# Moving vector work, loads and sums about in a TensorE-bound attention-and-experts kernel

## The chip, the cores and the metric

The kernel runs on one core of a Trainium2 chip. The metric is the device time of one execution in microseconds (us), the median of several runs; lower is better. Engines are named as the profile names them: PE is TensorE (PEld its weight loads), DVE is VectorE, ACT is ScalarE, POOL is GpSimd, SP is SyncE, which here only issues DMAs. The 16 runs of the kernel before lie within 0.4% of one another.

## The reference, cut to what matters

```python
def reference(...):
    # q, k, v: (8 batches, 8 heads, 576 tokens, 64), float32
    # sliding-window attention (window 128) with a distance bias per head
    x = attention(q, k, v)                  # then reshaped to 4608 tokens x 512
    logits = x @ w_gate                     # 8 experts
    P = exp(logits - logits.max())
    for _ in range(8):                      # Sinkhorn: rows and columns in turn
        P /= P.sum(1, keepdims=True) + 1e-09
        P /= P.sum(0, keepdims=True) + 1e-09
        P *= N / E
    out = 0
    for e in range(8):                      # every token goes to every expert
        h = maximum(x @ w1[e], 0)           # 512 -> 1024
        out += P[:, e:e+1] * (h @ w2[e])    # 1024 -> 512
    return out
```

Two facts follow from it. Routing weights need all tokens (column sums), so Sinkhorn cannot start before attention ends. And the eight dense experts are the bulk of the work.

## The kernel before

The kernel has these stages in time:

1. Attention, block by block, with expert 0 filled in wherever TensorE has room. Expert 0 does not need routing weights before its output is scaled, so six of its nine groups of 512 tokens are done here. Activations of a group are also written to DRAM (`xTd`), from where later experts read them.
2. Sinkhorn on VectorE and GpSimd, while TensorE does the other three groups of expert 0. The routing weights then go through DRAM (`PTd`) and come back broadcast to all partitions (`Pb`).
3. Expert 1, nine tasks of one group each, then experts 2 and 3, 4 and 5, 6 and 7 in pairs. Both layers use a Strassen (Winograd) form: seven products of half-size blocks for eight, paid for with sums and differences on VectorE. The names below: `xd` sums of activations, `ws` sums of first-layer weights, `T` sums of second-layer weights, `S` sums of hidden activations. A call `chunk(j, n)` is one eighth of the first layer of task `j`; it is woven into the second layer of the task before.

The result accumulates in `acc` in SBUF. `quad(g, rh, ch)` is one quarter (256 token rows by 256 columns) of a group. In the Winograd form one partial sum belongs to three of the four quarters: it is kept once, in quarter (1,1), and added to the others at the end (`settle`). For that, expert 0's result has to be scaled by its routing weight (`rescale`) and quarter (1,1) subtracted from two other quarters (`rebase`).

```python
        # Sinkhorn stage: four weight loads (2 MB in DRAM each), then eight iterations
        load_w1(1, msb); load_w2(1, msb); load_w1(2, msb); load_w2(2, msb)   # issued by GpSimd
        for it in range(ITERS):
            ...                                   # row sums on VectorE
            nc.gpsimd.partition_all_reduce(ca_sb, cs_sb, P, bass_isa.ReduceOp.add)
            ...
        for g in range(g0):                       # g0 = 6
            rebase(g, 1)                          # VectorE, 128x512
        load_x(f"0_{g0}", g0)                     # activations of groups 6 and 7 from DRAM
        load_x(f"0_{g0 + 1}", g0 + 1)
        e0_l1(g0)                                 # expert 0, first layer, group 6
        for g in range(g0 + 1, NG):
            e0_l1(g)
            if g < NG - 1:
                e0_l2(g - 1)
        # (cut) transposes of the routing weights -> PT_sb -> DRAM (PTd)
        e0_l2(NG - 2)
        load_w1(3, per)
        # (cut) read PTd back as Pb; weight sums of expert 1; first chunks between e0_l2(NG - 1)
        load_w2(3, per)
```

```python
    # (cut) inside an expert-1 task h; order = (1, 7, 5, 6, 2, 4, 3)
    for k in range(7):
        unit.product(order[k])                    # 8 matmuls of 256 columns
        chunk(j, k if k < 4 else k + 1)           # 8, 8, 8 or 4 matmuls of the next task, in turn
        if k == 0:
            unit.make_s(2)
            unit.gather(0)                        # VectorE: quarter (1,1) += product 1
        if k == 1: unit.gather(1, op=ALU.subtract)
        if k == 2: unit.gather(2, op=ALU.subtract)
        if k == 3: unit.gather(3)
        if k == 4:
            unit.make_s(4)
            unit.gather_far(0, 0, 0)              # ScalarE copy + accumulating DMA
        # (cut) k == 5, 6: two more gather_far; make_x of the task after next
        if k in (0, 1, 2, 4):
            rescale(4 * (h + 1) + (0, 1, 2, None, 3)[k])      # ScalarE, 128x512
        if k == 5:
            rebase(h + 1, 0)                      # VectorE, 128x512
            if h + 1 >= g0:
                rebase(h + 1, 1)
```

```python
    # weight sums and T tiles at a change of experts (h = first task of the expert)
    at(h - 2, 3, make_ws, e, 1); at(h - 2, 5, make_ws, e, 2)
    at(h - 2, 6, make_ws, e, 3); at(h - 1, 0, make_ws, e, 4)
    at(h, 3, make_t, p, 0); at(h, 6, make_t, p, 3)            # for pairs after the first
    at(h + 1, 1, make_t, p, 1); at(h + 1, 6, make_t, p, 2)
```

The softmax here doesn't subtract the row's maximum and nothing guards it: scores larger than these inputs give would overflow.

## Time and profile before

| | before |
|---|---|
| median, 16 runs | 1072.34 us (1069.83 to 1074.42) |
| profiled span | 1071.1 us |
| TensorE busy | 94% |
| attention ends (last gate matmul) | 211.1 us |
| first expert-1 product | 274.0 us |
| last matmul starts | 1061.3 us |

The first line is from the page of the kernel before: busy time of each engine, its share of the span, and instructions.

```profile
PE 1007.3 (94%) x9187; PEld 818.0 (76%) x9187; DVE 861.5 (80%) x1352; ACT 645.2 (60%) x1154; POOL 204.6 (19%) x211
```

94% looks full, but shares over the span say little here. The stage windows say more. Columns of the window view: stretch in us, its length, then busy time and (instructions) of PE, PEld, DVE, ACT, POOL, then the granted TensorE clock, the busy share of the DMA engines and their GB/s. The lines are of the kernel before.

```profile
275.00:300.00 25.00, 24.74 (x225) 21.64 (x223) 23.18 (x38) 20.27 (x37) 4.84 (x4) 1.00 0.48 112
300.00:325.00 25.00, 24.27 (x218) 20.89 (x217) 23.58 (x38) 20.09 (x37) 7.19 (x6) 1.00 0.60 117
325.00:350.00 25.00, 23.93 (x216) 20.64 (x214) 23.58 (x38) 19.88 (x37) 6.17 (x6) 1.00 0.63 126
350.00:375.00 25.00, 23.20 (x207) 19.81 (x205) 23.77 (x39) 19.44 (x36) 7.02 (x6) 1.00 0.64 127
375.00:400.00 25.00, 20.78 (x179) 17.19 (x178) 23.83 (x37) 15.93 (x29) 5.57 (x5) 1.00 0.64 137
400.00:425.00 25.00, 22.90 (x207) 19.93 (x205) 22.32 (x30) 14.03 (x25) 3.53 (x4) 1.00 0.71 138
...
450.00:475.00 25.00, 25.00 (x232) 22.40 (x230) 20.22 (x29) 15.40 (x29) 3.98 (x4) 1.00 0.42 96
...
600.00:625.00 25.00, 24.06 (x219) 21.10 (x217) 23.67 (x36) 14.62 (x27) 4.89 (x6) 1.00 0.93 180
```

Read the count beside the busy time of PE. In the steady paired stage (450 us) TensorE is busy 25.00 of 25 us and starts 232 matmuls. Up to 425 us it starts fewer, down to 179, while DVE is busy 22.3 to 23.8 us. Busy time alone hides part of this, because matmuls overlap: 218 against 232 matmuls is 6% less work, 24.27 against 25.00 us is 3%.

The length of one expert-1 task can be read from the SyncE timeline: it issues one load of `Pb` per task. Columns: start, duration, engine, line, operation, out<-in.

```profile
324.04 0.42 SPq L579 DMA_DIRECT2D Pb<-PTd  x1
337.30 0.42 SPq L579 DMA_DIRECT2D Pb<-PTd  x1
```

That is 13.26 us a task here (12.65 us in the tasks without a weight sum).

Between attention and expert 1 the waits of PE from 210 to 275 us, kernel before (waiter, line, what it waited for: us in total, times, longest), are:

```profile
PE psh L114 <- DMA xl<-xTd: 7.1, 1, 7.1
PE la L641 <- DVE xl L586: 2.6, 1, 2.6
```

And the chain that ended last, kernel before, runs through the DRAM round trip of the routing weights (start, us, what):

```profile
249.54 6.64 DMA PTd<-PT_sb
...
256.20 4.10 DMA Pb<-PTd
...
260.52 1.24 DVE xl L586
...
261.85 0.60 PE la L641 x4
```

The end of the kernel before, from its timeline. In brackets stands the idle time before and what ended it.

```profile
1045.71 20.70 SPq L76 DMA_DIRECT2D out_dram<-acc_hi  x20
...
1055.45 0.69 DVE L780 TENSOR_TENSOR acc_hi<-acc_hi 128x512 f32<-128x512 f32 x1 [2.82 <-DMA acc_hi<-st]
...
1057.93 1.92 PE L741 MATMUL M<-w2t,S 128*128 128x256 f16 x16 [3.13 <-DVE S L721]
...
1061.33 5.39 ACTq L76 DMA_DIRECT2D out_dram<-acc_hi  x4
```

A `settle` (L780) waits 2.8 us for an accumulating DMA, the last S tile stands behind it on VectorE, and TensorE waits 3.1 us for that tile. SyncE is still issuing stores at 1066.4 us.

### The profile page before, as it was taken

The numbers are of one execution on the slowest core, as the hardware profiler recorded it, in microseconds if no ns is written. First come the engines' busy times: TensorE is split into PE (matmuls) and PEld (weight loads), VectorE is DVE, ScalarE is ACT, GpSimd is POOL, SyncE is SP. The second block draws the span as 40 slices with busy tenths as digits, with TensorE's granted clock in tenths as the row PEclk, the third lists the DMA queues.
The fourth block names the chain that finished last, engine by engine and source line by source line (L and its number), as shares of the span: only waits on it lengthen the run. The fifth ranks groups of instructions, "written<-read, shape, count | busy, mean of one in ns | idle before, by whom it ended". The sixth has DMA issues, their size and how long they took to land.

```text
span 1071.1 us, 22451 instructions
## 1 busy us (share of the span) xinstructions
PE 1007.3 (94%) x9187; PEld 818.0 (76%) x9187; DVE 861.5 (80%) x1352; ACT 645.2 (60%) x1154; POOL 204.6 (19%) x211
## 2 busy tenths in 40 slices
PE   4899999789999989999999999999999999999995
PEld 2555555434788768888888888888888888888884
DVE  5777767565999998888888997888888988888874
ACT  3576666445787765665656555666655565655660
POOL 6323230020122221111111211111111111111111
PEclk9799999989999999999999999999999999999999
DMA  9977883194666566445334983344446635555545
GB/s 174 168 96 91 103 106 39 41 213 110 128 119 119 119 137 130 100 111 106 90 89 97 182 176 90 89 94 96 109 109 137 129 89 129 149 138 129 129 108 139
DMA packets 122071, 125.98 MB, mean 118 GB/s; under 512 B 46704, under 2 KB 97424, under 8 KB 121968
## 3 DMA queue, kind: packets, MB, share of 16 engines
q0 software_dynamic: 92720, 58.89, 40.0%
q1 hardware_dynamic: 28960, 65.40, 19.9%
q8 instruction: 72, 1.18, 0.5%
q10 hardware_dynamic: 288, 0.26, 0.1%
q14 instruction: 31, 0.25, 0.1%
HBM read 113.62 MB, written 14.30 MB: 119 GB/s over the span
## 4 chain that ended last, share of the span: by engine, by line
issue 58%; PE 21%; POOL 12%; DMA 3%; DVE 3%; ACT 2%; POOLq 0%; SPq 0%; DVEq 0%; ACTq 0%
POOL acc_lo L757 7%; PE psh L114 6%; PE psy L128 5%; POOL acc_hi L757 3%; PE psS L224 3%; PE psN L272 2%; PE M L741 1%; ACT pt L232 1%; DMA qf<-in_q_dram 1%; PE lb L641 1%; PE psT_q L193 1%; DMA acc_hi<-st 1%; PE psXT L312 1%; DMA PTd<-PT_sb 1%; PE psT_k L193 1%
## 5 line engine op out<-in xcount | busy, mean ns | idle before, releaser
L741 PEld LDWEIGHTS <-hT 128*128 128x128 f16 x2504 | 245.0, 98 | 28.4
L641 PEld LDWEIGHTS <-w1t 128*128 128x128 f16 x2016 | 196.9, 98 | 43.2 <-issue 19.0
L741 PE MATMUL M<-w2t,hT 128*128 128x256 f16 x1496 | 194.0, 273 | 0.0
L757 POOL DMA_DIRECT2D acc_lo<-st x72 | 85.8, 1211 | 441.7 <-ACT st L756 405.5
L641 PEld LDWEIGHTS <-ws 128*128 128x128 f16 x1512 | 147.8, 98 | 19.2 <-issue 1.8
L586 DVE TENSOR_TENSOR xl<-xl,Pb 128x1024 f16<-128x1024 f16 x126 | 153.4, 1217 | 5.9 <-DMA Pb<-PTd 5.9
L641 PE MATMUL la<-xl,w1t 128*128 128x256 f16 x1008 | 151.2, 273 | 2.6 <-DVE xl L586 2.6
L652 ACT ACTIVATE hT<-lc 128x512 f16<-128x512 f32 x126 | 75.3, 598 | 123.8 <-PE lc L641 118.5
L652 ACT ACTIVATE hT<-la 128x512 f16<-128x512 f32 x126 | 75.3, 598 | 112.7 <-PE la L641 112.7
L741 PE MATMUL M<-T,hT 128*128 128x256 f16 x1008 | 130.6, 273 | 0.0
L675 DVE TENSOR_TENSOR lc<-lb,m 128x512 f32<-128x512 f32 x126 | 88.0, 698 | 45.6 <-PE lb L641 45.5
L680 DVE TENSOR_TENSOR m<-lb,m 128x512 f32<-128x512 f32 x126 | 86.8, 689 | 36.0 <-PE lb L641 34.3
L741 PEld LDWEIGHTS <-S 128*128 128x128 f16 x1024 | 99.5, 98 | 19.5 <-DVE S L715 4.3
L666 ACT COPY lb<-la 128x512 f32<-128x512 f32 x126 | 71.9, 570 | 33.8 <-PE la L641 31.8
L652 ACT ACTIVATE hT<-lb 128x512 f16<-128x512 f32 x126 | 75.6, 600 | 14.3 <-PE lb L641 14.0
L652 ACT ACTIVATE hT<-m 128x512 f16<-128x512 f32 x126 | 78.6, 624 | 6.1 <-DVE m L680 6.0
L641 PE MATMUL lb<-xl,w1t 128*128 128x256 f16 x504 | 75.5, 272 | 5.6 <-DVE lc L675 5.4
L641 PE MATMUL lb<-xd,w1t 128*128 128x256 f16 x504 | 75.6, 272 | 5.2 <-DVE m L680 4.0
L232 ACT ACTIVATE pt<-psS 128x1024 f16<-128x1024 f32 (+2 forms) x80 | 68.2, 852 | 17.6 <-PE psS L224 16.4
L641 PE MATMUL lb<-xd,ws 128*128 128x256 f16 x504 | 75.6, 272 | 1.1 <-ACT lb L666 1.1
L641 PE MATMUL ld<-xd,ws 128*128 128x256 f16 x504 | 75.6, 273 | 0.0
L641 PE MATMUL lc<-xl,ws 128*128 128x256 f16 x504 | 75.6, 273 | 0.0
(86 smaller groups left out, 1512.1 us busy)
## 6 DMA issues: line engine op xcount, KB each, us to landing
xl<-xTd SPq DMA_DIRECT2D x66, 512.0 KB
acc_lo<-st POOLq DMA_DIRECT2D x72, 256.0 KB, 5.8
Pb<-PTd SPq DMA_DIRECT2D x63, 256.0 KB
acc_hi<-st POOLq DMA_DIRECT2D x33, 256.0 KB, 5.4
w2t<-in_moe_w_dram POOLq DMA_DIRECT2D x8, 1024.0 KB, 12.0
w1t<-in_moe_w_dram POOLq DMA_DIRECT2D x7, 1024.0 KB, 10.0
out_dram<-acc_lo SPq DMA_DIRECT2D x48, 128.0 KB
kf<-in_k_dram POOLq DMA_DIRECT2D x16, 288.0 KB, 5.6
```

Of the source, the lines that this page charges most:

```text
L114: nc.tensor.matmul(out=psh, lhsT=w1t[:, dt, P * ft : P * ft + P], rhs=x[:, dt, :], start=(dt == 0), stop=(dt == NDT - 1),)
L128: nc.tensor.matmul(out=psy, lhsT=hT[:, ft, P * ms : P * ms + P], rhs=w2ts[e][:, ft, :], start=(ft == 0), stop=(ft == NFT - 1),)
L224: nc.tensor.matmul(out=ps[0:nk, jj, :, 0:nq], lhsT=KT[:, 2 * half + jj, k0 : k0 + nk], rhs=QZ[:, 2 * half + jj, :, k0 : k0 + nq],)
L232: nc.scalar.activation(out=pt[0:nk, :, 0:nq], in_=ps[0:nk].rearrange("p a b q -> p (a b) q")[:, :, 0:nq], func=AF.Exp, scale=scale,)
L586: tt(out=x, in0=x, in1=Pbs[j].unsqueeze(1).to_broadcast([P, 2, GT]), op=ALU.mult)
L641: nc.tensor.matmul(out=ps[:, f, :], lhsT=a[:, kt, f0 : f0 + P], rhs=b[:, kt, :], start=(m in (1, 5) and f == 0 and kt == 0), stop=(kt == 1 ...
L652: nc.scalar.activation(out=hTs[j][:, f0 : f0 + 2, T2 * th : T2 * th + T2], in_=src, func=AF.Relu)
L666: nc.scalar.copy(out=lbanks["lb"], in_=lbanks["la"])
L675: tt(out=lbanks["lc"], in0=lbanks["lb"], in1=m5s[j], op=ALU.add)
L680: tt(out=m5s[j], in0=lbanks["lb"], in1=m5s[j], op=ALU.add)
L741: nc.tensor.matmul(out=ps[:, ms, :], lhsT=a[:, kt, P * ms : P * ms + P], rhs=b[:, kt, :], start=(new and ms == 0 and kt == 0), stop=(kt == ...
L757: nc.gpsimd.dma_start(out=quad(self.g, rh, ch), in_=st, accum_op=ALU.add)
```

## The change

The intent is to fill the holes of TensorE. The parts:

- Activations of groups 6 and 7 are loaded during attention.
- The four weight loads are issued behind the first four Sinkhorn all-reduces; expert 3's weights load later, inside expert 1.
- All rebases go. Quarter (1,1) of expert 0's scaled result is set apart and stored straight to the output, so the accumulator's quarter (1,1) starts from zero: its first gather is a ScalarE copy instead of a VectorE addition, and the final quarter is added to the output in DRAM by an accumulating DMA. Those come from GpSimd; the Trainium skill ("DMA: Bandwidth & Descriptors", section on SWDGE, HWDGE and iDMA) gives accumulation to GpSimd's DMAs only, and in the trace all 36 accumulating stores are POOL's.
- Weight sums and T tiles get new, spread places; one T tile shares memory so that the next pair's can be made early; one task (`plain`, the first of expert 3) runs its first layer without Strassen, so that its weight sums may come later.
- Expert 0's last layer-2 work is woven with the first chunks in half pieces.
- At the end rows are settled earlier, the last group but one is gathered without DMAs, and the last S tile is made before the settles of its own group.

The core of the diff, cut:

```diff
+                    if groups in (NHI // 4, NHI // 4 + 1):      # in the attention loop
+                        load_x(f"0_{groups}", groups)
 ...
-        load_w1(1, msb)
-        load_w2(1, msb)
-        load_w1(2, msb)
-        load_w2(2, msb)
 ...
             nc.gpsimd.partition_all_reduce(ca_sb, cs_sb, P, bass_isa.ReduceOp.add)
+            if it < 4:
+                (load_w1, load_w2)[it % 2](1 + it // 2, msb)
 ...
-        def rescale(blk):
-            nc.scalar.mul(acc(blk), acc(blk), Pe_sb[:, 0, blk : blk + 1])
-        def rebase(g, rh):
-            t = quad(g, rh, 1 - rh)
-            nc.vector.tensor_tensor(out=t, in0=t, in1=quad(g, 1, 1), op=ALU.subtract)
+        def set_apart(g, i):            # 128x256 to a staging tile, stored to out
+            ...
+            nc.scalar.mul(t, acc(blk)[:, HF:HD], Pe_sb[:, 0, blk : blk + 1])
+            store_from(t, blk, HF, HD)
+        def scale_rest(g, n):
+            ...
 ...
-        e0_l2(NG - 2)
-        load_w1(3, per)                 # now at task 1, and load_w2(3) at task 2
+        plain = first[3]
 ...
+            def first_gather(self):
+                nc.scalar.copy(out=quad(self.g, 1, 1), in_=banks[0])
 ...
+        def add_out(blk):
+            store_from(acc(blk)[:, HF:HD], blk, HF, HD,
+                       (nc.gpsimd, nc.gpsimd), accum_op=ALU.add)
 ...
+        W_SLOTS = {
+            2: ((-7, 2), (-6, 1), (-5, 2), (-4, 1)),
+            3: ((-2, 5), (-1, 5), (0, 1), (0, 5)),
+            4: ((-2, 0), (-2, 2), (-1, 0), (-2, 5)),
+            5: ((-2, 1), (-2, 5), (-2, 6), (-1, 0)),
+        }
+        T_SLOTS = {
+            2: ((-3, 3), (-2, 2), (1, -1), (2, -1)),
+            4: ((0, 1), (0, 5), (0, 3), (2, -1)),
+        }
 ...
+                if unit.last:
+                    put_row(g - 1, 1)
+                    put_row(g - 1, 0)
```

More of the change, by code (lines that the diff above doesn't have):

```diff
@@ L71, in acc, with store_from @@
         return acc_lo[:, blk, :] if blk < NHI else accs[1][:, blk - NHI, :]
-    def store(blk: int, c0: int = 0, c1: int = HD, engs=(nc.sync, nc.sync)):
+    def store_from(t, blk: int, c0: int, c1: int, engs=(nc.sync, nc.sync), **kw):
         for c, eng in enumerate(engs):
@@ L77, in store @@
                 out=out[t0 : t0 + HB, c0:c1].rearrange("(i r) d -> r i d", r=RT),
-                in_=acc(blk)[HB * c : HB * c + HB, c0:c1],
-            )
+                in_=t[HB * c : HB * c + HB],
+                **kw,
+            )
+    def store(blk: int, c0: int = 0, c1: int = HD, engs=(nc.sync, nc.sync)):
+        store_from(acc(blk)[:, c0:c1], blk, c0, c1, engs)
     P_sb = per.tile([P, NBLK, E], FP32, name="P_sb")
@@ L108, in x_dram, with load_x @@
         return xTd[P * g : P * g + P, :].rearrange("p (dt t) -> p dt t", dt=NDT)
+    xls: dict = {}
+    def load_x(key, g: int):
+        xls[key] = per.tile([P, NDT, GT], FP16, name=f"xl_{key}", tag="xl", bufs=2)
+        nc.sync.dma_start(out=xls[key], in_=x_dram(g))
     def l1_piece(e: int, g: int, ft: int, x, hT, ps_pool, tag: str, bufs: int):
@@ L126, in l2_mm, with l2_part @@
         )
-        for ft in range(NFT):
+        l2_part(e, ms, hT, psy, range(NFT))
+        return psy
+    def l2_part(e: int, ms: int, hT, psy, fts):
+        for ft in fts:
             nc.tensor.matmul(
@@ L134, in l2_mm @@
             )
-        return psy
     def new_hT(e: int, g: int, n: int, pool):
@@ L472 @@
         nc.sync.dma_start(out=identf, in_=identf_h.ap())
-        load_w1(1, msb)
-        load_w2(1, msb)
-        load_w1(2, msb)
-        load_w2(2, msb)
-        xls: dict = {}
-        def load_x(key, g: int):
-            xls[key] = msb.tile([P, NDT, GT], FP16, name=f"xl_{key}", tag="xl", bufs=2)
-            nc.sync.dma_start(out=xls[key], in_=x_dram(g))
         def quad(g: int, rh: int, ch: int):
@@ L524, in e0_l2 @@
                 nc.scalar.copy(out=acc(4 * g + ms), in_=psy)
-        def rescale(blk):
-            nc.scalar.mul(acc(blk), acc(blk), Pe_sb[:, 0, blk : blk + 1])
-        def rebase(g, rh):
-            t = quad(g, rh, 1 - rh)
-            nc.vector.tensor_tensor(out=t, in0=t, in1=quad(g, 1, 1), op=ALU.subtract)
+        c22: dict = {}
+        def set_apart(g, i):
+            if i == 0:
+                c22[g] = msb.tile([P, 2, HF], FP32, name=f"c22_{g}", tag="st", bufs=NST)
+            t = c22[g][:, i]
+            blk = 4 * g + 2 + i
+            nc.scalar.mul(t, acc(blk)[:, HF:HD], Pe_sb[:, 0, blk : blk + 1])
+            store_from(t, blk, HF, HD)
+        def scale_rest(g, n):
+            blk = 4 * g + n
+            c = slice(0, HF if n > 1 else HD)
+            nc.scalar.mul(acc(blk)[:, c], acc(blk)[:, c], Pe_sb[:, 0, blk : blk + 1])
         g0 = NHI // 4
-        for g in range(g0):
-            rebase(g, 1)
-        load_x(f"0_{g0}", g0)
-        load_x(f"0_{g0 + 1}", g0 + 1)
         e0_l1(g0)
@@ L542 @@
                 e0_l2(g - 1)
-        psP = mps.tile([P, 3, P], FP32, name="psP", tag="la")
+            load_x(g - g0 - 1, g - g0 - 1)
+        psP = mps.tile([P, 3, P], FP32, name="psP", tag="m3")
         CR = E * NBLK // 3
@@ L592, in make_xd @@
             e, g = tasks[j]
+            if j == plain:
+                return
             if n == 1:
@@ L659, in chunk @@
             e, g = tasks[j]
+            if j == plain:
+                if n == 0:
+                    hTs[j] = new_hT(e, g, (j + 2) % 3, msb if (j + 2) % 3 == 2 else per)
+                l1_piece(e, g, n, xls[j], hTs[j], mps, LB[n % 4], 1)
+                return
             dp, c = divmod(n, 4)
@@ L764, in make_t @@
         def make_t(e, n):
-            if n < 3:
+            if e == 1 and n == 0:
+                t = msb.tile([P, 2, KT2, HF], FP16, name="T01_1", tag="T1")
+                Ts[(1, 0)], Ts[(1, 1)] = t[:, 0], t[:, 1]
+            elif n < 3 and (e, n) not in Ts:
                 Ts[(e, n)] = msb.tile(
@@ L780, in settle, with put_row @@
             tt(out=t, in0=t, in1=quad(g, 1, 1), op=ALU.add)
-        def put_out(g):
-            settle(g, 1, 0)
-            store(4 * g + 2)
-            store(4 * g + 3)
-            settle(g, 0, 1)
-            store(4 * g)
-            store(4 * g + 1)
+        def put_row(g, rh):
+            settle(g, rh, 1 - rh)
+            for blk in (4 * g + 2 * rh, 4 * g + 2 * rh + 1):
+                store(blk, 0, HF if rh else HD)
+                if rh:
+                    add_out(blk)
+        def add_out(blk):
+            store_from(
+                acc(blk)[:, HF:HD], blk, HF, HD, (nc.gpsimd, nc.gpsimd), accum_op=ALU.add
+            )
         def make_x(j, part):
@@ L800, in make_x @@
                     make_xd(j, n)
-        for j in range(2):
-            load_x(j, tasks[j][1])
-            load_p(j)
+        load_p(0)
+        load_p(1)
+        for n in range(4):
+            e0_l2(NG - 2, range(n, n + 1))
+            if n < 2:
+                set_apart(0, n)
+            scale_rest(0, n)
         for n in (1, 3, 2, 4):
             make_ws(1, n)
-        for n in (0, 3, 1, 2):
+        for n in (0, 3):
             make_t(1, n)
-        for blk in range(4):
-            rescale(blk)
         for part in range(3):
             make_x(0, part)
-        for n in range(4):
-            e0_l2(NG - 1, range(n, n + 1))
-            if n:
-                chunk(0, n - 1)
-        load_w2(3, per)
-        rebase(0, 0)
-        make_x(1, 0)
-        chunk(0, 3)
-        chunk(0, 4)
-        chunk(0, 5)
-        make_x(1, 1)
-        chunk(0, 6)
-        make_x(1, 2)
-        chunk(0, 7)
+        for n in range(8):
+            ms, half = divmod(n, 2)
+            if half == 0:
+                psy = mps.tile([P, HD], FP32, name=f"psy_0_{4 * NG - 4 + ms}", tag=f"m{ms}")
+            l2_part(0, ms, hT0[NG - 1], psy, range(NFT // 2 * half, NFT // 2 * half + NFT // 2))
+            if half:
+                nc.scalar.copy(out=acc(4 * NG - 4 + ms), in_=psy)
+            chunk(0, n)
+            if n in (1, 2):
+                make_t(1, n)
+            if n in (3, 4, 6):
+                make_x(1, n // 2 - 1)
         unit = Unit(0)
@@ L833, in at @@
             due.setdefault((h, slot), []).append((f, args))
-        for e in range(2, E):
-            h = first[e]
-            if e == 2:
-                for n, m in enumerate((1, 2, 3, 4)):
-                    at(2 + n, 5, make_ws, e, m)
-                continue
-            at(h - 2, 3, make_ws, e, 1)
-            at(h - 2, 5, make_ws, e, 2)
-            at(h - 2, 6, make_ws, e, 3)
-            at(h - 1, 0, make_ws, e, 4)
+        W_SLOTS = {
[4 rows of a table added]
+        }
[3 more added lines that the diff above has]
+        }
+        for e in range(2, E):
+            for m, (dh, slot) in zip((1, 2, 3, 4), W_SLOTS[e if e < 4 else 4 + e % 2]):
+                at(first[e] + dh, slot, make_ws, e, m)
         for p in range(2, E, 2):
             h = first[p]
-            if p > 2:
-                at(h, 3, make_t, p, 0)
-                at(h, 6, make_t, p, 3)
-                at(h + 1, 1, make_t, p, 1)
-                at(h + 1, 6, make_t, p, 2)
-            else:
-                at(h, 1, make_t, p, 0)
-                at(h, 4, make_t, p, 3)
-                at(h, 6, make_t, p, 1)
-                at(h + 1, 4, make_t, p, 2)
-                at(8, -1, load_w1, 4, msb)
+            for n, (dh, slot) in zip((0, 3, 1, 2), T_SLOTS[min(p, 4)]):
+                at(h + dh, slot, make_t, p, n)
+            if p == 2:
+                at(1, 3, load_w1, 3, per)
+                at(2, 3, load_w2, 3, per)
+                at(8, 4, load_w1, 4, msb)
                 at(10, -1, load_w2, 4, msb)
@@ L891 @@
                     chunk(j, k if k < 4 else k + 1)
+                    if k in (0, 1, 2, 4):
+                        n = (2, 3, 0, None, 1)[k]
+                        scale_rest(h + 1, n)
+                    if k in (1, 4):
+                        set_apart(h + 1, k // 4)
                     if k == 0:
                         unit.make_s(2)
-                        unit.gather(0)
+                        unit.first_gather()
                     if k == 1:
@@ L899 @@
                     if k == 3:
+                        chunk(j, 4)
                         unit.gather(3)
+                        make_xs(h + 2, 0)
                     if k == 4:
                         unit.make_s(4)
+                        make_xd(h + 2, 1)
                         unit.gather_far(0, 0, 0)
                     if k == 5:
+                        make_x(h + 2, 1)
                         unit.gather_far(2, 1, 0)
                     if k == 6:
+                        Unit(h + 1).make_s(3)
+                        make_x(h + 2, 2)
                         unit.gather_far(1, 0, 1)
-                    if k == 3:
-                        chunk(j, 4)
-                        make_x(h + 2, 0)
-                    if k == 4:
-                        make_x(h + 2, 1)
-                    if k == 5:
-                        make_x(h + 2, 2)
-                    if k in (0, 1, 2, 4):
-                        rescale(4 * (h + 1) + (0, 1, 2, None, 3)[k])
-                    if k == 5:
-                        rebase(h + 1, 0)
-                        if h + 1 >= g0:
-                            rebase(h + 1, 1)
-                    if k == 6:
-                        Unit(h + 1).make_s(3)
                     extra()
@@ L934 @@
                 chunk(j, 1)
-                unit.gather(0)
+                if unit.pair:
+                    unit.gather(0)
+                else:
+                    unit.first_gather()
                 extra()
@@ L958 @@
                 if unit.last:
-                    put_out(g - 1)
+                    unit.make_s(4)
+                elif unit.e == E - 2 and g > 0:
+                    put_row(g - 1, 1)
+                    put_row(g - 1, 0)
                 extra()
@@ L967 @@
                 chunk(j, 0)
-                unit.gather(3)
+                if unit.pair:
+                    unit.gather(3)
+                else:
+                    unit.gather_far(3, 1, 1)
                 extra()
                 if end:
-                    unit.make_s(4)
+                    for blk in (4 * g + 2, 4 * g + 3):
+                        add_out(blk)
                     unit.product(4)
@@ L974 @@
                     settle(g, 1, 0)
-                    engs = (nc.sync, nc.gpsimd)
-                    store(4 * g + 2, engs=engs)
-                    store(4 * g + 3, engs=engs)
+                    for blk in (4 * g + 2, 4 * g + 3):
+                        store(blk, 0, HF)
                     unit.product(3)
@@ L980 @@
                     settle(g, 0, 1)
+                    engs = (nc.scalar, nc.sync)
                     for blk in (4 * g, 4 * g + 1):
-                        store(blk, HF, HD, (nc.scalar, nc.gpsimd))
+                        store(blk, HF, HD, engs)
                     unit.product(2)
@@ L985 @@
                     for blk in (4 * g, 4 * g + 1):
-                        store(blk, 0, HF, (nc.sync, nc.scalar))
+                        store(blk, 0, HF, engs)
                     break
@@ L1002 @@
                 chunk(j, 5)
-                unit.gather_far(2, 1, 0)
+                near = unit.e == E - 2 and g == NG - 2
+                (unit.gather if near else unit.gather_far)(2, 1, 0)
                 make_x(h + 2, 1)
@@ L1011 @@
                 chunk(j, 7)
-                unit.gather_far(1, 0, 1)
+                (unit.gather if near else unit.gather_far)(1, 0, 1)
                 load_next(h)
-                if unit.e == E - 2 and g > 0:
-                    put_out(g - 1)
                 extra()
```

## The prediction

> **What bounds the kernel now.** TensorE. In the stage windows from 425 to 600 us and 650 to 825 us it is busy 25.0 of every 25 us at clock 1.00, about 229 matmuls of 256 columns, 0.109 us each. The 7,056 Strassen-form matmuls of experts 1 to 7 are worth 770 us; the change removes none (one task is made plain: 32 matmuls of 512 columns for 56 of 256, about +0.8 us). So it gains only where TensorE stands still. The windows and the wait view show where:
>
> 1. 211.1 to 218.4 us: TensorE waits 7.1 us for `xl<-xTd`, the first activations of the expert-0 remainder, then runs at clock 0.50 until about 223 us (cost 2.3 us).
> 2. 249 to 274 us: routing weights go to DRAM and back (6.6 + 4.1 us in the chain of waits); TensorE waits 2.6 us, then runs the first expert-1 chunks with holes. The first expert-1 product starts at 274.0 us.
> 3. 275 to 425 us: VectorE is busy 23 to 24 of 25 us; about 140 matmuls are missing against the steady rate, 15 us. Worst is 375 to 400 us (53 missing), where weight sums and T tiles of the next experts fall together.
> 4. 600 to 650 and 825 to 875 us: about 2 us each, same cause.
> 5. The end: S4 waits behind a `settle` that waits for an accumulating DMA: TensorE idles 3.1 us; the last addition ends at 1062.3 us, the span at 1071.1 us.
>
> **What the change does, with its worth.**
> - Activations of groups 6 and 7 are loaded during attention: item 1 goes, 6.5 to 7 us. I expect the clock drop to stay: the clock falls at about 209.6 us, before the wait. (The Trainium skill, "TensorE: Matmul & The Clock Gate", Part 1, gives half rate after an idle window of about 3.4 us; the 0.50 here agrees.)
> - The first Sinkhorn all-reduce no longer stands behind four weight loads (VectorE waits 5.4 us there). Sinkhorn ends near 238 instead of 243 us; six rebases (3.7 us) leave VectorE; expert 3's load no longer competes with the DRAM round trip; expert 0's last layer-2 work is spread between the chunks. First expert-1 product: about 264 us, 9 to 11 us earlier, item 1 included.
> - Per expert-1 task VectorE loses one rebase (0.61 us) and one gather (0.68): about 12.0 falls to 10.7 us, against TensorE's 12.2. ScalarE gains a copy (0.58) and split scaling (about +0.4, an estimate from the 0.72 us of a full block): 10.3 to 11.2 us. Task time 12.75 to about 12.4 us. With the spread weight sums and the plain task, item 3's 15 us fall to 6 or 7.
> - Item 4: half, 2 us.
> - End: S4 early, no wait for the DMA, fewer late stores, but accumulating DMAs to DRAM (POOL-issued stores take about 5.7 us to land): net 4 to 5 us.
>
> **Sum.** About 10 + 8.5 + 2 + 4.5 - 0.8 = 24 to 27 us, nearly all on the critical path because each item is TensorE idle time. Predicted 1047 us, range 1037 to 1057. Chances: faster by over 2% (below 1051) 0.74, within 2% 0.25, slower 0.01.
>
> **What would show it.** No `xl` wait near 211 us; first expert-1 product near 264 us; VectorE and ScalarE about 22 of 25 us in the expert-1 stage; no slice below 215 matmuls around 375 to 400 us; no S4 wait at the end; last matmul to span end under 9 us.
>
> **What would make it wrong.** ScalarE over 90% in the expert-1 stage becoming the new wait; a longer stall before the first chunk, since less expert-0 work lies ahead of it; a tail held by accumulating DRAM DMAs or SyncE's store queue; or, the other way, stalls vanishing almost wholly (about 1038).

## The result

The changed kernel takes 1042.54 us (median of 8 runs, 1041.5 to 1043.01) against 1072.34 us: 29.8 us less. The ratio is 0.972, 95% interval 0.971 to 0.973. The prediction said 1047, with a range of 1037 to 1057.

The spans of the two profiles differ by 30.9 us. Cut at marks that both timelines have, the difference falls into five parts (length of the stretch in us):

| stretch | before | after | gain |
|---|---|---|---|
| end of attention to first expert-1 product | 62.9 | 51.9 | 11.0 |
| from there to the first S sum of the first pair | 131.8 | 120.6 | 11.2 |
| from there to the first S sum of the last pair task | 640.4 | 637.1 | 3.3 |
| from there to the start of the last matmul | 15.1 | 11.7 | 3.4 |
| from there to the end | 9.8 | 7.9 | 1.9 |

The page of the changed kernel, busy time and share:

```profile
PE 1000.9 (96%) x9163; PEld 817.4 (79%) x9163; DVE 841.1 (81%) x1318; ACT 648.2 (62%) x1176; POOL 235.0 (23%) x242
```

DVE lost 20 us of work and yet its share rose. The windows of the changed kernel (columns as above):

```profile
275.00:300.00 25.00, 25.00 (x231) 22.39 (x230) 22.53 (x37) 22.74 (x46) 9.60 (x9) 1.00 1.09 218
300.00:325.00 25.00, 25.00 (x232) 22.37 (x230) 22.96 (x38) 22.94 (x46) 7.55 (x7) 1.00 0.79 166
325.00:350.00 25.00, 25.00 (x232) 22.40 (x230) 23.38 (x38) 22.74 (x46) 7.67 (x7) 1.00 0.74 153
350.00:375.00 25.00, 23.24 (x201) 19.41 (x199) 21.53 (x32) 19.30 (x38) 6.45 (x6) 1.00 0.91 195
375.00:400.00 25.00, 25.00 (x207) 20.02 (x205) 21.64 (x31) 14.13 (x26) 5.70 (x5) 1.00 0.80 161
400.00:425.00 25.00, 25.00 (x231) 22.41 (x230) 20.45 (x30) 15.30 (x28) 3.57 (x3) 1.00 0.42 96
...
575.00:600.00 25.00, 25.00 (x230) 22.25 (x229) 24.58 (x36) 15.18 (x28) 5.30 (x5) 1.00 0.95 183
600.00:625.00 25.00, 24.29 (x222) 21.48 (x220) 22.57 (x32) 14.82 (x27) 4.52 (x4) 1.00 0.67 134
```

The expert-1 stage now starts 231 or 232 matmuls in 25 us, the full rate. The counts of 201 and 207 do not mean as much as before: the 32 matmuls of the plain task, with 512 columns each, fall in these two slices and count as 64. With that, 350 to 400 us lacks about 462 - 440 = 22 matmuls of 256 columns, 2.4 us at 0.109 us each, all of them in the first of the two slices. ACT is now at 22.7 to 22.9 us.

The loads of `Pb` in the SyncE timeline of the changed kernel:

```profile
324.65 0.43 SPq L590 DMA_DIRECT2D Pb<-PTd  x1
336.88 0.43 SPq L590 DMA_DIRECT2D Pb<-PTd  x1
```

A task takes 12.23 us, against 12.65 to 13.26.

Of PE's waits between 200 and 275 us the 7.1 us for `xl` is gone; one wait for the round trip is left. First the waits of the changed kernel, then its timeline at that point:

```profile
PE la L654 <- DVE xl L597: 2.0, 1, 2.0
```

```profile
239.89 0.32 SPq L564 DMA_DIRECT2D PTd<-PT_sb  x1
...
244.36 0.81 SPq L590 DMA_DIRECT2D Pb<-PTd  x2
...
247.80 1.23 DVE L597 TENSOR_TENSOR xl<-xl,Pb 128x1024 f16<-128x1024 f16 x1 [3.95 <-DMA Pb<-PTd]
...
249.08 0.60 PE L654 MATMUL la<-xl,w1t 128*128 128x256 f16 x4 [2.03 <-DVE xl L597]
```

In these profiles SyncE's next issue is that of `Pb`, which has to wait until `PTd` is complete; so the two issue times show the first half of the round trip: 4.5 us here, 6.6 us before. The whole way from the issue of `PTd` to the scaling takes 7.9 us, before 11.0.

The end of the changed kernel, from its timeline:

```profile
1025.61 11.53 SPq L76 DMA_DIRECT2D out_dram<-acc_hi  x13
1026.34 1.22 DVE L739 TENSOR_TENSOR S<-hT,S 128x2048 f16<-128x2048 f16 x1
...
1028.92 1.91 PE L759 MATMUL M<-w2t,S 128*128 128x256 f16 x16
...
1032.32 4.24 ACTq L76 DMA_DIRECT2D out_dram<-acc_hi  x4
```

The last S tile is ready before TensorE needs it (no bracket at 1028.92), and SyncE's last stores are issued at 1037.1 us.

### The profile page after: what moved, and what is told of

Its sections match the earlier page's. It is cut to its first block, busy times and chain, and to the rows that moved or that the text cites. A ratio compares the mean times of both kernels' runs of the same rounds, so it can differ in the third digit from the quotient of the medians.

```text
span 1040.2 us, 22521 instructions
## 1 busy us (share of the span) xinstructions
PE 1000.9 (96%) x9163; PEld 817.4 (79%) x9163; DVE 841.1 (81%) x1318; ACT 648.2 (62%) x1176; POOL 235.0 (23%) x242
## 5 line engine op out<-in xcount | busy, mean ns | idle before, releaser
L759 PEld LDWEIGHTS <-hT 128*128 128x128 f16 x2504 | 245.0, 98 | 29.8
L654 PEld LDWEIGHTS <-w1t 128*128 128x128 f16 x1984 | 194.2, 98 | 30.0 <-issue 5.8
L654 PE MATMUL la<-xl,w1t 128*128 128x256 f16 x992 | 149.0, 273 | 2.0 <-DVE xl L597 2.0
L759 PEld LDWEIGHTS <-S 128*128 128x128 f16 x1024 | 100.2, 98 | 11.6
```

The source lines that it names most:

```text
L654: nc.tensor.matmul(out=ps[:, f, :], lhsT=a[:, kt, f0 : f0 + P], rhs=b[:, kt, :], start=(m in (1, 5) and f == 0 and kt == 0), stop=(kt == 1 ...
L759: nc.tensor.matmul(out=ps[:, ms, :], lhsT=a[:, kt, P * ms : P * ms + P], rhs=b[:, kt, :], start=(new and ms == 0 and kt == 0), stop=(kt == ...
```

## The experiments

Twelve kernels, all correct. Each was timed beside the kernel before on the same chip: the medians of before were 1071.64 us for e1 to e4, 1072.26 for e5 to e8 and 1071.96 for e9 to e12. The changed kernel was not timed again; the medians of before moved by up to 0.7 us. Apart from the timing, each profile was cut at three marks, because the end of attention lies anywhere from 207.7 to 211.6 us in these profiles, even for kernels that change nothing up to there. Differences of 1 or 2 us in medians of four or five runs are therefore weak, the same difference between marks inside the profiles less so. All lengths in us.

| kernel | median | ratio to before (95%) | end of attention to first expert-1 product | from there to last matmul | from there to end |
|---|---|---|---|---|---|
| before | 1072.34 | 1 | 62.9 | 787.3 | 9.8 |
| after | 1042.54 | 0.972 (0.971 to 0.973) | 51.9 | 769.4 | 7.9 |
| e1 before + early x | 1067.93 | 0.9971 (0.9944 to 0.9997) | 58.9 | 786.4 | 10.5 |
| e2 e1 + loads in Sinkhorn | 1068.67 | 0.9977 (0.9944 to 1.001) | 58.8 | 787.2 | 10.2 |
| e3 after, late x | 1048.87 | 0.9791 (0.9762 to 0.9819) | 58.4 | 770.1 | 7.8 |
| e4 after, loads first | 1041.93 | 0.9729 (0.9694 to 0.9764) | 52.5 | 769.7 | 8.0 |
| e5 after, DVE work back | 1049.28 | 0.9787 (0.9771 to 0.9802) | 51.2 | 777.2 | 8.1 |
| e6 after, ACT work more | 1044.73 | 0.9742 (0.9728 to 0.9757) | 51.4 | 772.4 | 8.2 |
| e7 before + spread sums | 1065.07 | 0.9941 (0.9924 to 0.9958) | 63.2 | 780.5 | 7.3 |
| e8 after, no plain task | 1045.09 | 0.9744 (0.9725 to 0.9762) | 51.6 | 773.2 | 7.9 |
| e9 after, expert 3 loaded early | 1049.21 | 0.9783 (0.9766 to 0.98) | 59.8 | 769.6 | 8.1 |
| e10 after, old slots | 1042.48 | 0.9726 (0.971 to 0.9743) | 51.7 | 771.9 | 7.7 |
| e11 after, old end | 1045.65 | 0.9752 (0.9739 to 0.9766) | 51.7 | 770.5 | 10.7 |
| e12 try to do better | 1044.89 | 0.9746 (0.973 to 0.9763) | 50.9 | 774.6 | 8.6 |

### From attention to expert 1: e1, e2, e3, e4, e9

**e1: the early activations alone, on the kernel before.**

```diff
+                    if groups in (NHI // 4, NHI // 4 + 1):
+                        load_x(f"0_{groups}", groups)
 ...
-        load_x(f"0_{g0}", g0)
-        load_x(f"0_{g0 + 1}", g0 + 1)
```

> The kernel before with one part of the change alone: groups 6 and 7 of the activations are loaded during attention. Theory: the wait for xl is only the first of two obstacles in series. Behind it the routing weights still leave Sinkhorn at 243 us and the six rebases at 247 us, so the DRAM round trip starts only about 2 us earlier than before (249.5). Expected: the 7.1 us wait near 211 us gone, but the time only about 2 us lower (1070), the rest turning into a longer TensorE wait before the first expert-1 chunk (2.6 to about 6 us or more). Rival: TensorE time saved there is simply saved; then the time falls by 7 to 10 us (1062 to 1065).

Measured: 3.7 us faster than before, 4.0 us between the marks. The wait of 7.1 us is gone, but more than 3 us of it comes back. The gain is more than the 2 us expected and far less than the 7 to 10 of the rival: the two obstacles are in series, as said. But what comes back is only in part the longer wait that was expected: TensorE stands still for 2.1 us before the transposes and 2.0 us before the first chunk (where the kernel before waited 2.6 us), and just behind that its clock is at 0.50 for 3.4 us, from 256.4 us, which takes another 1.7 us.

**e2: e1, and the weight loads behind the all-reduces.**

```diff
-        load_w1(1, msb)
-        load_w2(1, msb)
-        load_w1(2, msb)
-        load_w2(2, msb)
 ...
+            if it < 4:
+                (load_w1, load_w2)[it % 2](1 + it // 2, msb)
```

> The same, and the four weight loads of experts 1 and 2 moved behind the first four Sinkhorn all-reduces. Theory of two obstacles in series: Sinkhorn now ends near 238 us, rebases at 242 us, the round trip starts at 242.5 us, 7 us earlier than before; the time falls by 7 to 8 us (about 1065), far more than the early load alone. Rival (the all-reduce delay hardly matters): no more than 1 us better than the early load alone.

Measured: no gain over e1 at all (58.8 against 58.9 us between the marks). The theory fell. Its first half came true: the last Sinkhorn step starts at 237.8 us, not 242.2, and the round trip at 242.5, not 246.8 us. But it ends no sooner. The timelines of e1 and of e2, GpSimd and SyncE only, show why:

```profile
241.80 0.79 POOL L96 DMA_DIRECT2D w1t<-in_moe_w_dram  x1
...
246.84 0.33 SPq L552 DMA_DIRECT2D PTd<-PT_sb  x1
...
250.48 0.32 SPq L579 DMA_DIRECT2D Pb<-PTd  x1
```

```profile
241.49 0.76 POOL L96 DMA_DIRECT2D w1t<-in_moe_w_dram  x1 [4.11 <-PE psh L120]
...
242.51 0.33 SPq L550 DMA_DIRECT2D PTd<-PT_sb  x1
...
250.81 0.32 SPq L577 DMA_DIRECT2D Pb<-PTd  x1
```

`PTd`, 144 KB, was issued 4.3 us apart in the two kernels and was complete at the same time, about 9 us after the issue of expert 3's first weight load, and within 0.6 us of the landing of that load (250.0 us in e1, 250.6 us in e2). That was a new suspect, tested below as e9.

**e3: the changed kernel without the early activations.**

```diff
-                    if groups in (NHI // 4, NHI // 4 + 1):
-                        load_x(f"0_{groups}", groups)
 ...
+        load_x(f"0_{g0}", g0)
+        load_x(f"0_{g0 + 1}", g0 + 1)
         e0_l1(g0)
```

> The changed kernel with the early load of groups 6 and 7 undone (they are loaded after attention, as in before), everything else kept. Theory A (the idle wait of 7 us is what lowers the clock): the wait of about 7.3 us returns and with it 4 to 5 us at clock 0.50, so about +9.7 us, near 1052. Theory B (my prediction: the drop comes from the sparse TensorE work at 206 to 211 us, before the wait[...]): the wait returns but the clock may stay at 1.00, about +7.3 us, near 1050.

Measured: 6.3 us slower than the changed kernel, 6.5 us between the marks, in number nearer to theory B. So the early load is worth 6.5 us in the changed kernel and only 4.0 alone. On the clock: in 13 of the 14 profiles (before, after, e1 to e12) the granted clock falls to 0.50 between 206.0 and 209.8 us, where attention runs out and TensorE works in short bursts. It does so in e3, where theory B had hoped for 1.00, and in e1, e2, e4 to e6 and e8 to e12, which have no wait for `xl`. So the wait is not its cause.

The one profile without this drop is that of the changed kernel. It did not help that profile: its transposes came 2.5 us sooner after the end of attention than in e6 (27.7 against 30.2 us), but its first product did not (51.9 against 51.4 us). `PTd` was issued at 239.9 us, while the last of the four weight loads was still landing (until 242.6 us), and took 4.5 us; in e6 it was issued as that load landed, and took 3.0 us. TensorE waited 2.0 us for the routing weights, and then the clock fell after all, for 3.4 us. The window of the changed kernel (columns as above):

```profile
249.75:253.17 3.42, 3.42 (x15) 1.81 (x13) 2.10 (x5) 1.74 (x3) 0.00 (x0) 0.50 0.00 0
```

Such a second drop, of 3.4 to 6.8 us, also goes with the wait for the routing weights in e1, e2 and e9, though not with the 2.6 us of the kernel before or the 2.0 us of e4. It can be added up: the stretch from the end of attention to the first expert-1 product is idle time of TensorE, plus half of its busy time at clock 0.50, plus a rest of 48 to 49 us in all 14 profiles. Idle time and loss to the clock (estimates from the matmul and clock records) are 11.6 + 2.5 us before, 6.0 + 4.0 in e1, 6.1 + 4.0 in e2, 7.8 + 2.2 in e3, 6.9 + 4.8 in e9, 2.0 + 2.3 in e4 and 2.0 + 1.7 in the changed kernel. So what e3 loses is nearly all waiting.

**e4: the changed kernel with the weight loads ahead of Sinkhorn.**

```diff
-            if it < 4:
-                (load_w1, load_w2)[it % 2](1 + it // 2, msb)
 ...
+        load_w1(1, msb)
+        load_w2(1, msb)
+        load_w1(2, msb)
+        load_w2(2, msb)
         for it in range(ITERS):
```

> The changed kernel with the four weight loads put back ahead of the Sinkhorn loop. Theory: the first all-reduce waits again until 218.7 us, Sinkhorn ends about 5 us later, and as TensorE reaches the transposes of the routing weights at 238.6 us, it stands still for about 4.6 us there: near 1047. Rival (Sinkhorn has slack, other work fills): within 1 us of 1042.5.

Measured: no slower (1041.93 us, runs from 1039.4 to 1045.4), and 0.6 us between the marks. The theory fell again. TensorE does wait 2.0 us for the routing weights before the transposes, but as the weight loads have finished by then, `PTd` completes 2.0 us after its issue (4.5 us in the changed kernel), and that gives it back. The timeline of e4:

```profile
241.42 0.33 SPq L566 DMA_DIRECT2D PTd<-PT_sb  x1
...
243.45 0.81 SPq L592 DMA_DIRECT2D Pb<-PTd  x2
```

Together with e2: moving these four loads, and ending Sinkhorn 5 us sooner, gains nothing that the times show, and between the marks 0.6 us, or up to 1.3 us against e5, e6, e8, e10 and e11, which share e4's clock drop.

**e9: the changed kernel with expert 3's weights loaded at the old place.**

```diff
+        load_w1(3, per)                 # behind the issue of PTd
 ...
+        load_w2(3, per)
-                at(1, 3, load_w1, 3, per)
-                at(2, 3, load_w2, 3, per)
```

> The changed kernel with the loads of expert 3's weights put back where they stood: the first just behind the issue of the routing weights' DRAM round trip, the second just before the first expert-1 product. Earlier runs showed that an earlier Sinkhorn end gains nothing (e4, e2) and that the changed kernel without the early activations still reaches its first expert-1 product 4.5 us sooner than before, counted from the end of attention (e3). Theory: that rest is this load, 2 MB that stand in front of the round trip in the DMA engines: the way from the first DMA of the round trip to the first scaled activations goes from about 6 to 8 us to 10 or 11 us, and the time rises by 3 to 4 us (about 1046). Rival: the rest comes from the six rebases taken out or from the spread layer-2 work; then within 1 us of 1042.5.

Measured: 6.7 us slower, 7.9 us between the marks, about twice what was expected. The timeline of e9:

```profile
241.84 0.76 POOL L100 DMA_DIRECT2D w1t<-in_moe_w_dram  x1 [4.49 <-PE psh L124]
...
242.49 0.32 SPq L564 DMA_DIRECT2D PTd<-PT_sb  x1
...
251.82 0.81 SPq L592 DMA_DIRECT2D Pb<-PTd  x2
```

The small write of the routing weights takes 9.3 us beside the load, 4.5 us or less without it, and TensorE stands still for 6.9 us; during this wait the clock falls, which costs more time after it. This is the second obstacle of e1 and e2. The other candidates for this stretch, the rebases taken out and the half pieces of layer 2, were not tried alone. But in this stretch they are the main difference between e2 (58.8 us) and e9 (59.8 us), so with expert 3's load at its old place they gain nothing; what they are worth with it away was not tried.

### The expert-1 stage: e5, e6, e7, e8

**e5: VectorE's work put back.** One gather and two half-width additions per task.

```diff
-                        unit.first_gather()
+                        nc.vector.tensor_copy(out=quad(g, 1, 1), in_=banks[0])
 ...
                         unit.gather_far(2, 1, 0)
+                        for _ in range(2):
+                            nc.vector.tensor_tensor(out=dm, in0=dm, in1=dm, op=ALU.subtract)
```

> The changed kernel with the VectorE work that it took out of the expert-1 stage put back, and nothing else: the first gather of each of the eight tasks is a VectorE copy (0.68 us) instead of a ScalarE copy, and two VectorE additions of 256 columns on a scratch tile (about 0.66 us together, results unused) stand where the rebase stood. Theory: VectorE is what bound the expert-1 stage, so its busy time goes to 25 of 25 us there, TensorE gets holes again, and the time rises by 4 to 6 us (1046.5 to 1048.5). Rival: the stage gained from the new order and the spread sums; then less than 1.5 us.

Measured: 6.7 us slower, 7.8 us from the first expert-1 product to the last matmul. One window of e5, to be held against the same window of the changed kernel (232 matmuls):

```profile
325.00:350.00 25.00, 23.51 (x213) 20.40 (x211) 23.90 (x40) 19.89 (x41) 7.24 (x6) 1.00 0.71 149
```

VectorE is what bound the stage, with the new order and the spread sums in place too. It did not go to 25 of 25 us as expected: TensorE has holes here with VectorE busy 23.3 to 23.9 us, about as in the kernel before. That share is no fixed limit: in e7 it is 24.3 to 24.5 us in each of the same slices from 300 to 375 us, and from 575 to 600 us of the changed kernel VectorE is busy 24.58 us while TensorE still starts 230 matmuls.

**e6: more work for ScalarE.**

```diff
                         unit.gather_far(2, 1, 0)
+                        nc.scalar.copy(out=dm, in_=dm)      # 128x256, scratch
```

> The changed kernel with one more ScalarE copy of 256 columns (about 0.5 us, on a scratch tile) in each of the eight expert-1 tasks, which takes ScalarE from about 91% to about 95% busy there. Theory: ScalarE at 91% still has slack and TensorE bounds the stage: within 1 us of 1042.5. Rival (my warning in the prediction, ScalarE becomes the new wait): 2 us or more slower.

Measured: 2.2 us slower, 3.0 us between the marks: the rival's answer. Eight copies of about 0.5 us are 4 us of work, and three quarters of it reach the end. One window of e6:

```profile
325.00:350.00 25.00, 24.73 (x226) 21.84 (x224) 22.79 (x37) 22.75 (x47) 7.16 (x7) 1.00 0.69 149
```

ACT is busy 22.75 us, just as in the changed kernel without the extra copy (22.74), and TensorE starts 226 matmuls instead of 232. So ScalarE had no room left at 91%, at least at the one place in its queue where the copy was tried. The changed kernel has TensorE, ScalarE and nearly VectorE at their limits in this stage at once.

**e7: the spread sums, T tiles and the plain task alone, on the kernel before.**

```diff
-            at(h - 2, 3, make_ws, e, 1)          # and the other fixed places
+        W_SLOTS = {...}                          # as in the change
+        T_SLOTS = {...}
+        plain = first[3]                         # and its three uses
```

> The kernel before with only the new places of the weight sums and T tiles and the plain task (and the shared T tile that lets one T be made early). Theory: the losses where the experts change (375 to 425 us, 600 to 650, 825 to 875) shrink without any VectorE work being removed: 4 to 6 us faster (1066 to 1068). Rival: VectorE is full in the expert-1 stage, so sums moved into it cost there what they save later; then only the later two transitions gain, 2 to 3 us (about 1070).

Measured: 7.2 us faster than before, 6.8 us between the marks. Of that, 5.9 us lie between the first expert-1 product and the first S sum of the first pair (125.9 against 131.8 us). That is the theory's side, and a little above its size. The rival fails: the sums find room in the expert-1 stage even where VectorE seemed full. From 325 to 350 us VectorE goes from 23.58 to 24.35 us, and TensorE keeps its 216 matmuls. (This profile also ends 2.5 us sooner after the last matmul, which the edit does not touch. Part of this is the clock, which is at 0.50 for 3.4 us from 1046.3 us: its last matmuls take longer, while the stores go on.)

**e8: no plain task.**

```diff
-        plain = first[3]
+        plain = -1
-            3: ((-2, 5), (-1, 5), (0, 1), (0, 5)),
+            3: ((-2, 3), (-2, 5), (-2, 6), (-1, 0)),
```

> The changed kernel with the one plain task put back into Strassen form, for which expert 3's four weight sums have to stand earlier, where they stood before. Theory: the plain task costs TensorE 0.8 us and buys the spreading of the sums; without it VectorE is crowded around 370 to 385 us and the time is 1 to 3 us higher (1043.5 to 1045.5). Rival: VectorE has room by now, and the kernel gets 0.8 us faster (1041.7).

Measured: 2.5 us slower, 3.8 us between the marks. Giving up Strassen for one task, with the later places of the sums that this allows, pays, at the upper end of what was expected or above it.

### Later changes of experts and the end: e10, e11

**e10: old places of the sums for experts 4 to 7.**

```diff
-            4: ((-2, 0), (-2, 2), (-1, 0), (-2, 5)),
-            5: ((-2, 1), (-2, 5), (-2, 6), (-1, 0)),
+            4: ((-2, 3), (-2, 5), (-2, 6), (-1, 0)),
+            5: ((-2, 3), (-2, 5), (-2, 6), (-1, 0)),
 ...
-            4: ((0, 1), (0, 5), (0, 3), (2, -1)),
+            4: ((0, 3), (0, 6), (1, 1), (1, 6)),
```

> The changed kernel with the weight sums and T tiles of experts 4 to 7 at their old places. Theory: the two later changes of experts lose again what they lost before, about 3.4 us more than in the changed kernel (about 1046). Rival (the gain there comes from the new order of other work): within 1 us.

Measured: the time does not tell (1042.48 us; its profile has attention end 3.4 us early). The marks say 2.5 us. The distance from one pair's S sum to the next, 24.45 us in the steady stage, says the same: over the three pair tasks around each change of experts it grows by 1.1 and 1.2 us against the changed kernel. So the new places are worth about 2.3 us together. Of the rest of the 3.3 us in the paired stage, about half lies in the first pair task (24.04 us before, 23.55 in the changed kernel) and half in the last pair, where the old kernel settles and stores: one of its pair tasks took 25.66 us there, all of the changed kernel's 24.45 or 24.46 until the last. e7, with the new places but the old settles and stores, has the same 25.66 us in its last pair.

**e11: the old end.**

```diff
-                if unit.last:
-                    put_row(g - 1, 1)
-                    put_row(g - 1, 0)
 ...
-                if unit.last:
-                    unit.make_s(4)
-                elif unit.e == E - 2 and g > 0:
+                if unit.e == E - 2 and g > 0:
 ...
+                    unit.make_s(4)
                     unit.product(4)
 ...
-                near = unit.e == E - 2 and g == NG - 2
+                near = False
```

> The changed kernel with the end put back: the rows of the last group but one are settled and stored late, its last two gathers go through accumulating DMAs again, and S4 of the last group is made after them. The split output (accumulating stores) stays. Theory: TensorE waits about 3 us for S4 again: 3 to 4 us slower (about 1046). Rival (the accumulating stores to DRAM set the end of the changed kernel): within 1 us.

Measured: 3.1 us slower. The size is what was expected, the mechanism is not. The timeline of e11:

```profile
1027.87 13.78 SPq L76 DMA_DIRECT2D out_dram<-acc_hi  x16
...
1030.23 1.92 PE L759 MATMUL M<-w2t,S 128*128 128x256 f16 x16 [0.23 <-DVE S L739]
```

TensorE waits only 0.2 us for the S tile. What grows is the drain, from 7.9 to 10.7 us (7.7 to 8.6 us in the other versions of the changed kernel): the stores of the last group but one are issued late, and SyncE's queue of 16 stores ends at 1041.7 us (1037.1 in the changed kernel). So the order of settles and stores is worth 2.8 us through SyncE's queue. The 3.1 us wait of the old kernel, for an accumulating DMA that took 8 us to land, did not come back with the old order; what else took it away was not separated.

### e12: a try to do better

```diff
-            chunk(0, n)                          # behind each half piece of layer 2
+            for c in {2: (0,), 3: (1,), 4: (2,), 5: (3, 4), 6: (5,), 7: (6, 7)}.get(n, ()):
+                chunk(0, c)
 ...
-            store_from(t, blk, HF, HD)
+            store_from(t, blk, HF, HD, (nc.gpsimd, nc.gpsimd))
```

> A try to beat the changed kernel with two small edits. First, two more half pieces of expert 0's last layer-2 work run ahead of the first expert-1 chunk, where the profile of the changed kernel shows a 2 us wait for the routing weights. Second, the stores of the set-apart quarters are issued from GpSimd instead of SyncE, where they stand for 7 us in front of the loads of the next activations and routing weights (VectorE waits 2.5 us for those near 367 us). If both are real: 2 to 3 us faster (about 1040). In runs where the clock is low after attention the first wait is only about 0.5 us, and then the gain is 1 to 2 us. If GpSimd's queue holds up the gathers instead: slower.

Measured: 2.4 us slower than the changed kernel; the try failed. The first edit gave 0.3 to 1.0 us (50.9 between the marks, against 51.2 to 51.9). The second did harm. The timeline of e12:

```profile
306.17 0.51 ACT L540 ACTIVATE c<-acc_lo,Pe_sb 128x256 f32<-128x256 f32 x1 [3.48 <-DMA out_dram<-c]
...
309.43 0.60 PE L654 MATMUL lb<-xd,ws 128*128 128x256 f16 x4 [2.97 <-ACT lb L684]
```

The staging tile `c` belongs to a ring of five, and the stores from GpSimd free it later: ScalarE waits 3.5 us for such a store, and TensorE 3.0 us for ScalarE. In a stage where ScalarE is full, its queue is not the place to wait on a DMA. The changed kernel remains the best of the fourteen as far as the times tell (e4 and e10 are not to be told from it).

## Why the prediction was right, point by point

The time, 1042.54 us, lies in the range and on the side of "faster". The central value was 4.5 us too slow, and the terms came out as follows.

- **Attention to expert 1: right in size, wrong in one of its reasons.** Predicted 9 to 11 us and the first product near 264 us; measured 11.0 us and 262.9 us. The early activations are worth 6.5 us in place (e3). But the step "The first Sinkhorn all-reduce no longer stands behind four weight loads ... Sinkhorn ends near 238 instead of 243 us" happened as said and gained nothing (e2, e4). What gained is the half sentence behind it, "expert 3's load no longer competes with the DRAM round trip": undoing that costs 6.7 us (e9), part of it through the clock. These worths do not add up, since each obstacle hides part of the other (e1: 4.0 us alone).
- **The clock: right in general.** "I expect the clock drop to stay" holds in all other kernels with early activations; the profile of the changed kernel happened to have no drop there, but one of 3.4 us at 249.8 us, and gained nothing in this stretch. What the prediction cites from the Trainium skill ("TensorE: Matmul & The Clock Gate", Part 1) agrees with the 0.50, but the idle window of the same passage is not what came before this drop, since TensorE was idle for no more than about 1.0 us at a time.
- **The expert-1 stage: mechanism right, size off, and this is the term that was mis-sized.** The step "Task time 12.75 to about 12.4 us" and "item 3's 15 us fall to 6 or 7" left about 8.5 us of gain, less 0.8 for the plain task. The stretch gained 11.2 us: a task takes 12.23 us, TensorE's own time, and about 2.4 us of the 15 are left. Both causes named are shown: putting VectorE's work back costs 6.7 us (e5), and the spread sums alone bring 5.9 us in this stretch on the old kernel (e7). The predicted 12.4 us left 0.2 us a task over TensorE's 12.2 for waits on VectorE and ScalarE; there were none from 275 to 350 us, with ScalarE at 91 to 92% and VectorE at 90 to 94% busy. The worths of e5 and e7 add up to more than the 11.2 us, so these two causes overlap.
- **"ScalarE over 90% in the expert-1 stage becoming the new wait"**: it did not in the changed kernel, but e6 shows that there was no room left where it was tried.
- **Later changes of experts: right mechanism, a little small.** Predicted 2 us; the new places give 2.3 us (e10), and 3.3 us in all, with half a microsecond each from the first pair task and the last pair.
- **The end: right in size, half right in mechanism.** Predicted 4 to 5 us; measured 5.3 (3.4 to the last matmul, 1.9 after it). The wait for S4 went as said. But the order of settles and stores acts through SyncE's queue of stores, not through S4 (e11). The accumulating stores to DRAM, named as a risk, take about 5 us to land and do not set the end: the last of them are issued at about 1032 us, 8 us before it.
- **One of the signs was badly chosen**: "no slice below 215 matmuls" counted matmuls of 512 columns as one; the slices with the plain task show 201 and 207. Counted in 256 columns, 375 to 400 us is full, as predicted, but 350 to 375 us has about 209 and lacks 22.

## What to carry to other kernels

When one engine bounds a kernel, list the places where it stands still and price each change by the hole it fills; but two obstacles in series hide each other, so the worth of removing one must be asked with the other still there. Where TensorE waits, look at its clock after the wait too: a drop adds to the price. A small DMA on the critical path should not be issued beside a bulk load that can wait. And an engine at 91% busy may be full: test the room that is left by adding a little work before moving more to it.

## What the Trainium skill lacked or had wrong

- "DMA: Bandwidth & Descriptors", section on queues, rings and completion order, says that each DMA engine goes round-robin between its queues packet by packet, from which one would expect a small transfer to pass a large one. Measured: the 144 KB write `PTd` took 8.3 us (e2) and 9.3 us (e9) to completion beside a weight load of 2 MB from another queue and was done 0.2 us after that load had landed; beside the same load it took 6.7 us in the kernel before and 6.9 us in e7, and was done 2.9 and 2.8 us ahead of it; it took 4.5 us beside the last 2.7 us of such a load (changed kernel) and 2.0 to 3.2 us with the load landed (e4, e3, e10, e11). The page has no figure for a small transfer beside a large one.
- "Perfetto Trace Analysis", section on identifying the most-contended engine, takes the busy share of VectorE and ScalarE as a fair measure of how near they are to their limit. Here ScalarE had no room left at 22.75 of 25 us (91%): with more work given to it (e6) the share stayed and the stage grew longer. VectorE held TensorE up at 23.3 to 23.9 us (e5), and did not at 24.58 us in another stage (changed kernel).
- "TensorE: Matmul & The Clock Gate", Part 1, names an idle window of about 3.4 us for the drop to half rate, and further on short idle times between groups of matmuls that make the clock go back and forth. Here the clock fell to 0.50 between 206.0 and 209.8 us in 13 of 14 profiles while TensorE was not idle but worked in short bursts (busy 1.6 to 2.4 us of the 3.4 us before the drop, and idle for about 1.0 us at the longest), and once, with the same instructions, it did not fall there. The page gives no figure for how much sparse work keeps the clock up.
